# Retention attention into a top-1 mixture of experts: two matmul widths, shorter bodies and a new order of the helper steps

## The chip, the cores and the metric

The kernel runs on one core of a Trainium2 chip. The metric is the device time of one execution in microseconds, lower is better.

## The reference, cut to what matters

```python
# q, k, v: 8 batches x 8 heads x 576 positions x 64
scores = matmul(q, k.T) / sqrt(64)
gamma  = 1 - 2.0 ** (-5 - arange(8))                  # per head
ret    = scores * where(rel >= 0, gamma ** rel, 0)    # rel = row - column
x      = matmul(ret, v)  -> (4608 tokens, 512)

logits = normalize(x) @ normalize(expert_emb).T / tau
e      = argmax(logits)                               # one of 8 experts
gate   = softmax(logits)[e]
h      = maximum(x[tokens of e] @ w1[e], 0)           # 512 -> 1024
out[tokens of e] = gate * (h @ w2[e])                 # 1024 -> 512
```

## The kernel before, in words

**Attention.** 36 tiles of 128 tokens are worked in 18 steps of two tiles (`for s in range(HS)`, L858). The SyncE queue loads a tile's queries and keys (`qkt`) and its keys and values (`kvt`) into pools of seven buffers (`NLOAD = 7`). At the start of step s it loads the two tiles five ahead (L861 to L863). TensorE forms scores (`emit_A`), applies the carried state (`emit_QT`), multiplies with the values (`emit_O`) and updates the state (`emit_U`); the result is transposed (`emit_T`), copied by ScalarE into the two-buffer pool `my` and stored row by row into the scratch array `xd` (`emit_rows`). The routing of four tiles at a time is spread over later steps by a list of jobs (`at((step, place), ...)`, run by `do`).

**Between.** Once slots are known, GpSimd gathers the tokens of an expert from `xd` (`gather`), SyncE turns each gathered tile by a transposing DMA (`turn`), and a `join` puts the two 16-bit halves of each number back together. ScalarE then makes the high part of a number (`...hi`, a rounding cast) and VectorE the low part (`...lo`, number minus high part). Each product runs as three matmuls: high x high, high x low, low x high. Expert 0 is computed plainly.

**Experts 1 to 7** (L1289). The first product (512 to 1024) runs by a seven-product scheme in the manner of Strassen: sums and differences of weight quarters (`sumS1` to `sumS4`, VectorE) and of token quarters (`xsums`, VectorE), each split into high and low parts (`whi`, `wlo`, `xhi`, `xlo`). An expert's tokens lie in five tiles, each cut in two halves, so a matmul has one column for each pair of slots, 320 at most. The width is chosen at run time: the count of tokens, in steps of 16 above 512, is read into a TensorE register, and `products` writes its body once for each width of `WIDTHS`, under `tc.If` on that register (`pick`, L1033). Six calls of `products` make the 168 matmuls of an expert, in bodies of 24, 24, 48, 36, 24 and 12. Their results are turned into the hidden layer: `outs_mid`, `outs_last`, `hhi` (ScalarE, with ReLU), `hlo` (VectorE), `plus` (VectorE) and `copy` (ScalarE).

The second product (1024 to 512) is `mm2`: per tile of 128 tokens 8 blocks of 3 matmuls of 512 columns. `evac` scales by the gate on ScalarE and `scatter` (GpSimd) writes the rows out. The fifth tile runs only if the expert has more than 512 tokens (`tc.If(width > 0)`).

Within an expert all engines follow the written order of the program. While expert e runs, expert n = e + 1 is prepared between its pieces: weight quarters are loaded (`wload`, three buffers `wraw`), tokens gathered and turned, then joined on GpSimd (`join(n, i, nc.gpsimd.tensor_copy)`), summed and split. `wn` and `wnext` are the second product's weights, loaded in four parts.

Of the kernel before, what the change touches and what calls it, by code (L numbers as in the profile page):

```python
# [9 lines left out]
F32 = mybir.dt.float32  # L10
# [8 lines left out]
P = 128  # L19
# [5 lines left out]
DM = H * D  # L25
# [17 lines left out]
HW = CAP // 2  # L43
STEP = 16
WMIN = 2 * 2 * P
WIDTHS = (256, 288, 304, 320)
TOP = tuple((2 * w - WMIN) // STEP for w in WIDTHS)
KT = 9
NLOAD = 7
# [48 lines left out]
def retention_moe(ctx: ExitStack, tc: tile.TileContext, qk, kv, embT, tau, w1, w2, cst, out):  # L98
# [423 lines left out]
    with ExitStack() as att:  # L522
# [3 lines left out]
        a1 = att.enter_context(tc.tile_pool(name="a1", bufs=1))  # L526

        pmp = att.enter_context(tc.tile_pool(name="pmp", bufs=4))
        csb = ap.tile([P, _CST.shape[1] - _FIRST], F32, name="csb")
        pop = att.enter_context(tc.tile_pool(name="pop", bufs=1, space=PSUM))  # L530
        po = pop.tile([P, 2, 2, 2 * P], F32, name="po")
# [228 lines left out]

        def emit_rows(t, bank):

            xw = my.tile([P, DM], F32, name="y")
            nc.scalar.copy(
                xw.bitcast(U16).rearrange("p (h n) -> p h n", h=2),
                bank.bitcast(U16).rearrange("p (n h) -> p h n", h=2),
            )
            nc.sync.dma_start(out=xd[t * P : (t + 1) * P, :], in_=xw.bitcast(U16))
# [69 lines left out]
        for i in range(3):  # L838
            at((15, 1), lambda i=i: turn(0, i))
            at((16, 3), lambda i=i: join(0, i, nc.gpsimd.tensor_copy))  # L840
        at((17, 0), lambda: (xhi0(0), xlo0(0)))
        at((17, 1), lambda: (xhi0(1), xhi0(2), xlo0(1), xlo0(2)))

        def loads(t):
            if t < NT:
                load_qk(t)
                load_kv(t)
# [10 lines left out]
        for s in range(HS):  # L858
            t, u = 2 * s, 2 * s + 1
            do(s, 0)  # L860
            if s > 0:  # L861
                loads(t + NLOAD - 2)
                loads(u + NLOAD - 2)  # L863
            scale_v(t + 2, nc.gpsimd)
            scale_v(u + 2, nc.gpsimd)
            for k in (t + 2, u + 2):
                if k < KT:
                    decay(k)
            if 0 < s < HS - 1:
                emit_A(t + 2)  # L870
                emit_A(u + 2)
            do(s, 1)
            emit_QT(t)
            emit_QT(u)
            emit_U(u)
            emit_O(t)
            emit_O(u)
            if s == 0:
                emit_A(2)
                turn_k(2)  # L880
                emit_A(3)
                turn_k(3)
            do(s, 1.5)
            if s > 0:
                emit_T(u - 2, pa[3])
                emit_T(t - 2, prow)
            if 0 < s < HS - 1:
                emit_rows(u - 2, pa[3])
                emit_sq(u - 2, pa[3])
            emit_U(t + 2)  # L890
            emit_X(t)
            emit_X(u)
            do(s, 2)
# [29 lines left out]
    with ExitStack() as moe:  # L923
# [201 lines left out]
        gather(1, 0)  # L1125
        gather(1, 3)
        mm1_in(5, 0, q0[5])
        on(prow)
        gates_out()
        gather_gates(0)  # L1130
        out0_hi(4, 0, q0[4])
        wn.hi(1)
        out0_lo(4, 0, q0[4])
        wn.lo(1)
        turn(0, 3)
        wload(1, "A11")
        turn(0, 4)
        mm1_in(6, 0, q0[6])
        out0_hi(5, 0, q0[5])
        wn.hi(2)  # L1140
        out0_lo(5, 0, q0[5])
# [15 lines left out]
        wlo("A11")  # L1157
        join(0, 3)
        mm2(b0[0], 0, (4, 5))
        sumS3()  # L1160
        xhi0(3)
        xlo0(3)
        xg.pop((0, 3))
        gather(1, 1)
        gather(1, 4)
        mm2(b0[0], 0, (6, 7), end=7)
        evac(0, 0, b0[0])
        scatter(0, 0)
        join(0, 4)
        sumS1()  # L1170
        mm2(b0[1], 1, (0, 1), begin=0)
        whi("S3")
        xhi0(4)
        wlo("S3")
        mm2(b0[1], 1, (2, 3))
        whi("A22")
        xlo0(4)
        xg.pop((0, 4))
        gather(1, 2)
        turn(1, 1)  # L1180
        on(prow)
        count_beyond()
        mm2(b0[1], 1, (4, 5))
# [105 lines left out]
        for e in range(1, NE):  # L1289
# [25 lines left out]
            if more:  # L1315
                wload(n, "A21")
                gather_gates(n)

            products(
                width,  # L1320
                (3, 0, VA[0], 0),
                (3, 1, VA[1], 0),
                (7, 0, YA[0], 0),
                (7, 1, YA[1], 0),
                (1, 2, XB[0], 1),
                (1, 3, XB[1], 1),
                (5, 2, VB[0], 1),
                (5, 3, VB[1], 1),
            )
# [5 lines left out]
            if more:  # L1335
# [1 line left out]
                for i in range(3):  # L1337
                    turn(n, i)

            products(  # L1340
                width,
                (4, 0, YA[0], 0),
                (4, 1, YA[1], 0),
                (2, 2, XB[0], 0),
                (2, 3, XB[1], 0),
                (6, 2, YB[0], 0),
                (6, 3, YB[1], 0),
            )
            hhi(4, 0, YA[0])
            hhi(5, 0, YA[1])  # L1350
            if more:
                whi("A11")
                wlo("A11")
            hlo(4, 0, YA[0])
            hlo(5, 0, YA[1])
            outs_mid((2, 3), XB, YB)
            if more:
                sumS3()
                sumS1()
                for i in range(3):  # L1360
                    join(n, i, nc.gpsimd.tensor_copy)

            products(width, (3, 2, VB[0], 0), (3, 3, VB[1], 0), (7, 2, YB[0], 0), (7, 3, YB[1], 0))
            if more:
                outs_last((2, 3), VB, YB, lambda: whi("S1"), lambda: (wlo("S1"), sumS2("A21")))
            else:
                outs_last((2, 3), VB, YB)

            o = (bank[4], bank[5], bank[6], bank[7], bank[4])
            wnext = Split(n, 1, w2f) if more else None  # L1370
            mm2(o[0], 0, (0, 1), begin=0)
            if more:
                whi("S2")
            mm2(o[0], 0, (4, 5))
            if more:
                wlo("S2")
                whi("S3")
            products(width, (4, 2, YB[0], 0), (4, 3, YB[1], 0))
            if more:
                wlo("S3")  # L1380
                wload(n, "A12")
            hhi(6, 0, YB[0])
            hhi(7, 0, YB[1])
            hlo(6, 0, YB[0])
            hlo(7, 0, YB[1])
            mm2(o[0], 0, (2, 3))
            if more:
                xsums(n, 0)
                xhi(n, 0, "abc")
            mm2(o[1], 1, (0, 1), begin=0)  # L1390
            if more:
                xlo(n, 0, "abc")
                ready(n, 0)
                turn(n, 3)
                whi("A22")
            mm2(o[1], 1, (4, 5))
            if more:
                xsums(n, 1)
                xhi(n, 1, "abc")
            mm2(o[1], 1, (2, 3))  # L1400
            if more:
                wlo("A22")
# [6 lines left out]
            if more:  # L1409
                xsums(n, 2)  # L1410
                xhi(n, 2, "abc")
            mm2(o[1], 1, (6, 7), end=7)
            evac(e, 1, o[1])
            scatter(e, 1)
            if more:
                xlo(n, 2, "abc")
                ready(n, 2)
            mm2(o[2], 2, (0, 1), begin=0)
            if more:
                whi("A12")  # L1420
                wlo("A12")
            mm2(o[2], 2, (2, 3))
            if more:
                sumS4()
                wnext.load(0)
                whi("S4")
            mm2(o[2], 2, (4, 5))
            if more:
                join(n, 3, nc.gpsimd.tensor_copy)
                wlo("S4")  # L1430
                wnext.load(1)
                wnext.load(2)
            mm2(o[2], 2, (6, 7), end=7)
            evac(e, 2, o[2])
            scatter(e, 2)
            if more:
                xsums(n, 3)
                xhi(n, 3, "abc")
            mm2(o[3], 3, (0, 1), begin=0)
            if more:  # L1440
                join(n, 4, nc.gpsimd.tensor_copy)
                xlo(n, 3, "abc")
                ready(n, 3)
# [193 lines left out]
```

## Time and profile before

| | before |
|---|---|
| median of 3 timed runs | 614.42 us (610.39 to 614.44) |
| profiled execution | 606.46 us |
| its span, first to last instruction | 604.6 us |
| TensorE matmul busy | 566.0 us, 94%, 5156 matmuls |
| VectorE busy | 435.8 us, 72% |
| ScalarE busy | 312.1 us, 52% |
| GpSimd busy | 245.1 us, 41% |
| mean granted TensorE clock | 0.982 |

A share is the busy time over the span. Matmuls overlap in a pipeline, so 94% does not say that TensorE is at its peak. The profiled execution is one run of its own; the timed ones were taken apart from it. The attention takes about the first quarter of the span, the experts 1 to 7 from 219.5 us on.

### The profile page before, as it was taken

Reading aid. Unit: us, or ns where it says so; the run is one execution under the profiler, and the core shown is the slowest. Engines: PE = TensorE matmul, PEld = TensorE weight load, DVE = VectorE, ACT = ScalarE, POOL = GpSimd, SP = SyncE. Lnnn points to the kernel's source line nnn. Section 1 sums busy time; section 2 is a strip of 40 time slices with the busy share of each in tenths; the row PEclk is TensorE's granted clock in tenths of the full one; section 3 lists DMA queues with packets and bytes.
Section 4 is the critical chain, followed back from the end, with each engine's and each line's share of the span. In section 5 each row is a group of like instructions: output and inputs, shape, how many; then the busy total and the mean of one; then the engine's idle time right before and its main releaser. Section 6 shows DMA issues by size and latency. Waiting matters only on the chain.

```text
span 604.6 us, 13187 instructions
## 1 busy us (share of the span) xinstructions
PE 566.0 (94%) x5156; PEld 504.0 (83%) x5156; DVE 435.8 (72%) x880; ACT 312.1 (52%) x610; POOL 245.1 (41%) x218
## 2 busy tenths in 40 slices
PE   8999999999998999899899899979689999999996
PEld 7888888888887999789788878977589888889985
DVE  2777687887777777986996598759847976987500
ACT  2345454554645785537536544736465656447411
POOL 4652233226447236237525623570374137331011
PEclk9999999999998999999999899979989999999999
DMA  8898998997467549176655906572665449353001
GB/s 295 331 326 315 371 352 328 381 352 240 160 175 176 131 147 260 49 178 210 104 139 159 236 25 157 193 159 54 175 204 95 105 151 268 43 157 113 3 36 46
DMA packets 83085, 111.84 MB, mean 185 GB/s; under 512 B 48135, under 2 KB 48427, under 8 KB 82992
## 3 DMA queue, kind: packets, MB, share of 16 engines
q1 hardware_dynamic: 75312, 90.55, 51.1%
q0 software_dynamic: 7680, 19.95, 9.4%
q8 instruction: 70, 1.15, 0.8%
q14 instruction: 23, 0.19, 0.1%
HBM read 81.10 MB, written 19.94 MB: 167 GB/s over the span
## 4 chain that ended last, share of the span: by engine, by line
PE 39%; DVE 21%; issue 17%; DMA 9%; ACT 7%; POOL 3%; SPq 2%; POOLq 0%; DVEq 0%; ACTq 0%
PE pa L127 16%; PE po L127 10%; PE pst L127 6%; PE prow L127 5%; DVE w0f L989 4%; DVE graw L453 4%; DVE hs L1018 3%; DVE wraw L971 3%; DMA wraw<-w 3%; DMA qkt<-qk 2%; POOL out L1085 2%; DVE st L1031 2%; SPq L411 2%; PE pa L131 1%; DVE wxf L989 1%
## 5 line engine op out<-in xcount | busy, mean ns | idle before, releaser
L1085 POOL DMA_INDIRECT out<-y,sid x40 | 42.3, 1058 | 203.9 <-ACT y L1081 129.9
L127 PE MATMUL po<-w2f,hs 128*128 128x512 f32 x408 | 94.2, 389 | 0.0
L127 PEld LDWEIGHTS po<-w2f,hs 128*128 128x128 f32 x408 | 76.4, 188 | 15.8
L127 PE MATMUL pst<-w2f,hs 128*128 128x512 f32 (+1 forms) x336 | 80.2, 385 | 5.9 <-DVE hs L1018 4.6
L127 PEld LDWEIGHTS pst<-w2f,hs 128*128 128x128 f32 x336 | 60.4, 188 | 19.6 <-DVE hs L1018 7.2
L641 POOL TENSOR_TENSOR kvt<-kvt,cs 128x512 f32<-128x512 f32 x35 | 37.7, 1083 | 65.8 <-DMA kvt<-kv 44.4
L193 DVE TENSOR_TENSOR w2f<-wraw,w2f 128x1024 fp32r<-128x1024 f32 x32 | 39.2, 1224 | 32.2 <-ACT w2f L189 32.2
L418 POOL COPY graw<-graw 128x1024 uint16<-128x1024 uint16 x33 | 51.9, 1599 | 25.0 <-DMA graw<-graw 25.0
L986 ACT CAST w0f<-wraw 128x1024 fp32r<-128x1024 f32 x28 | 29.2, 1046 | 58.2 <-DVE wraw L971 58.2
L463 ACT CAST xxf<-graw 128x128 fp32r<-128x128 f32 x70 | 31.8, 460 | 51.4 <-DVE graw L453 51.4
L127 PE MATMUL pa<-xxf,w0f 128*128 128x256 f32 (+3 forms) x348 | 52.4, 305 | 5.3 <-ACT w2f L189 1.7
L127 PEld LDWEIGHTS pa<-xxf,w0f 128*128 128x128 f32 x348 | 49.6, 199 | 6.4 <-ACT w2f L189 1.9
L989 DVE TENSOR_TENSOR w0f<-wraw,w0f 128x1024 fp32r<-128x1024 f32 x28 | 44.8, 1600 | 12.2 <-ACT w0f L986 12.2
L658 DVE TENSOR_TENSOR pm<-pa,tri 128x512 f32<-128x512 f32 x64 | 40.1, 682 | 12.1 <-PE pa L127 12.1
L453 DVE TENSOR_TENSOR graw<-graw 128x128 f32<-128x128 f32 x140 | 44.6, 360 | 3.2 <-ACT graw L418 2.0
L397 POOL DMA_INDIRECT gt<-gd,gid x40 | 39.8, 996 | 16.7 <-issue 11.9
L127 PE MATMUL prow<-w2f,hs 128*128 128x512 f32 x192 | 46.0, 389 | 0.0
L127 PE MATMUL pa<-qkt 64*128 64x128 f32 x576 | 43.0, 284 | 2.2 <-DMA qkt<-qk 1.5
L989 DVE TENSOR_TENSOR wxf<-wraw,wxf 128x1024 fp32r<-128x1024 f32 x21 | 26.0, 1236 | 26.1 <-ACT wxf L986 26.1
L127 PEld LDWEIGHTS prow<-w2f,hs 128*128 128x128 f32 x192 | 36.0, 188 | 7.7
L971 DVE TENSOR_TENSOR wraw<-wraw 128x1024 f32<-128x1024 f32 x28 | 40.4, 1441 | 2.6 <-DMA wraw<-w 1.9
L127 PEld LDWEIGHTS pa<-qkt 64*128 64x128 f32 x576 | 38.0, 190 | 5.1 <-DMA qkt<-qk 1.8
(196 smaller groups left out, 1138.8 us busy)
## 6 DMA issues: line engine op xcount, KB each, us to landing
wraw<-w SPq DMA_DIRECT2D x64, 512.0 KB, 4.7
qkt<-qk SPq DMA_DIRECT2D x36, 512.0 KB, 7.2
kvt<-kv SPq DMA_DIRECT2D x32, 512.0 KB, 7.9
xd<-y SPq DMA_DIRECT2D x36, 256.0 KB, 4.2
kvt<-kv SPq DMA_DIRECT2D x4, 256.0 KB, 6.3
gt<-gd,gid POOLq DMA_INDIRECT x40, 5.6
out<-y,sid POOLq DMA_INDIRECT x40, 3.1
graw<-xd,gid POOLq DMA_INDIRECT x26, 5.7
```

What stands on the lines that cost most here:

```text
L127: pe[:] = [nc.tensor.matmul(*args, **kw)]
L193: nc.vector.tensor_tensor(out=self.to[:, 1, c * 1024 : (c + 1) * 1024], in0=self.raws.pop(c), in1=hi.bitcast(F32), op=ALU.subtract,)
L397: nc.gpsimd.indirect_dma_start(out=g[:, i : i + 1], out_offset=None, in_=gd[:, :], in_offset=bass.IndirectOffsetOnAxis(ap=gid[:, a : a + 1 ...
L418: copy(t[:, :DM].bitcast(U16).rearrange("p (n h) -> p h n", h=2), t[:, XO : XO + DM].bitcast(U16).rearrange("p (h n) -> p h n", h=2),)
L453: nc.vector.tensor_tensor(out=v[:, 2 * k : 2 * k + 2], in0=a, in1=b, op=ALU.subtract)
L463: nc.scalar.copy(x[:, 0], u)
L641: eng.tensor_tensor(out=v, in0=v, in1=gneg[:, t % KT].unsqueeze(2).broadcast_to([P, H, D]), op=ALU.mult)
L658: nc.vector.tensor_tensor(out=pm[:, h], in0=banks[h].rearrange("p (c n) -> p c n", c=NP), in1=m.unsqueeze(1).broadcast_to([P, NP, P]), op= ...
L971: nc.vector.tensor_tensor(out=raw[n], in0=raw[a], in1=raw[b], op=op)
L986: nc.scalar.copy(wop[n][:, 0], raw[n])
L989: nc.vector.tensor_tensor(out=wop[n][:, 1], in0=raw[n], in1=wop[n][:, 0].bitcast(F32), op=ALU.subtract)
L1085: sc = nc.gpsimd.indirect_dma_start(out=out[:, :], out_offset=bass.IndirectOffsetOnAxis(ap=sid[:, a : a + 1], axis=0), in_=ys[i], in_offse ...
```

## The change

It has six parts: two widths (296 and 320) in place of four; the calls of 48 and 36 matmuls cut into two each, so that no body exceeds 24; the joins of experts 2 to 7 on ScalarE; a new order of `hlo`, `wlo`, `whi`, `sum`, `xhi`, `xlo` and weight loads between the pieces of the second product; in the attention, loads of the next tiles written ahead of the same step's row stores, which get three buffers of their own; around expert 0, a later place for the gates and an earlier one for the last tokens' joins and parts.

```diff
-WIDTHS = (256, 288, 304, 320)
+WIDTHS = (296, 320)
...
+        rowp = att.enter_context(tc.tile_pool(name="rowp", bufs=3))
...
-            xw = my.tile([P, DM], F32, name="y")
+            xw = rowp.tile([P, DM], F32, name="xw")
...
-        at((17, 0), lambda: (xhi0(0), xlo0(0)))
-        at((17, 1), lambda: (xhi0(1), xhi0(2), xlo0(1), xlo0(2)))
+        at((17, 1), lambda: (xhi0(0), xhi0(1), xlo0(0), xlo0(1)))
+        at((17, 1.5), lambda: (xhi0(2), xlo0(2)))
...
             do(s, 0)
-            if s > 0:
-                loads(t + NLOAD - 2)
-                loads(u + NLOAD - 2)
...
                 turn_k(3)
+            if s + 1 < HS:
+                loads(t + NLOAD)
+                loads(u + NLOAD)
             do(s, 1.5)
...
-        on(prow)
-        gates_out()
-        gather_gates(0)
         out0_hi(4, 0, q0[4])
...
         wload(1, "A11")
+        mm1_in(6, 0, q0[6])
+        on(prow)
+        gates_out()
+        gather_gates(0)
         turn(0, 4)
-        mm1_in(6, 0, q0[6])
...
         mm2(b0[0], 0, (4, 5))
-        sumS3()
         xhi0(3)
+        join(0, 4)
         xlo0(3)
...
+        sumS3()
         mm2(b0[0], 0, (6, 7), end=7)
+        xhi0(4)
         evac(0, 0, b0[0])
         scatter(0, 0)
-        join(0, 4)
-        sumS1()
-        mm2(b0[1], 1, (0, 1), begin=0)
         whi("S3")
-        xhi0(4)
-        wlo("S3")
-        mm2(b0[1], 1, (2, 3))
-        whi("A22")
         xlo0(4)
...
+        mm2(b0[1], 1, (0, 1), begin=0)
+        sumS1()
+        wlo("S3")
+        whi("A22")
+        mm2(b0[1], 1, (2, 3))
...
-            products(
-                width,
-                (3, 0, VA[0], 0),
...
+            products(width, (3, 0, VA[0], 0), (3, 1, VA[1], 0), (7, 0, YA[0], 0), (7, 1, YA[1], 0))
+            products(width, (1, 2, XB[0], 1), (1, 3, XB[1], 1), (5, 2, VB[0], 1), (5, 3, VB[1], 1))
...
+            products(width, (4, 0, YA[0], 0), (4, 1, YA[1], 0), (2, 2, XB[0], 0), (2, 3, XB[1], 0))
+            products(width, (6, 2, YB[0], 0), (6, 3, YB[1], 0))
             hhi(4, 0, YA[0])
             hhi(5, 0, YA[1])
             if more:
                 whi("A11")
-                wlo("A11")
             hlo(4, 0, YA[0])
             hlo(5, 0, YA[1])
+            if more:
+                wlo("A11")
             outs_mid((2, 3), XB, YB)
             if more:
                 sumS3()
                 sumS1()
-                for i in range(3):
-                    join(n, i, nc.gpsimd.tensor_copy)
+                join(n, 0)
 
             products(width, (3, 2, VB[0], 0), (3, 3, VB[1], 0), (7, 2, YB[0], 0), (7, 3, YB[1], 0))
-            if more:
-                outs_last((2, 3), VB, YB, lambda: whi("S1"), lambda: (wlo("S1"), sumS2("A21")))
-            else:
-                outs_last((2, 3), VB, YB)
-
+            outs_last((2, 3), VB, YB)
...
+            if more:
+                whi("S1")
             mm2(o[0], 0, (0, 1), begin=0)
             if more:
-                whi("S2")
+                whi("S3")
+                wlo("S1")
+                sumS2("A21")
             mm2(o[0], 0, (4, 5))
...
             products(width, (4, 2, YB[0], 0), (4, 3, YB[1], 0))
...
             hhi(6, 0, YB[0])
             hhi(7, 0, YB[1])
+            if more:
+                whi("S2")
+                xsums(n, 0)
             hlo(6, 0, YB[0])
             hlo(7, 0, YB[1])
             mm2(o[0], 0, (2, 3))
             if more:
-                xsums(n, 0)
                 xhi(n, 0, "abc")
+                wlo("S2")
             mm2(o[1], 1, (0, 1), begin=0)
             if more:
+                join(n, 1)
                 xlo(n, 0, "abc")
                 ready(n, 0)
                 turn(n, 3)
-                whi("A22")
             mm2(o[1], 1, (4, 5))
             if more:
+                xhi(n, 1, "a")
                 xsums(n, 1)
-                xhi(n, 1, "abc")
+                xhi(n, 1, "bc")
...
                 ready(n, 2)
+                whi("A22")
             mm2(o[2], 2, (0, 1), begin=0)
             if more:
+                wlo("A22")
                 whi("A12")
+            mm2(o[2], 2, (2, 3))
+            if more:
                 wlo("A12")
-            mm2(o[2], 2, (2, 3))
-            if more:
                 sumS4()
                 wnext.load(0)
-                whi("S4")
+                wnext.load(1)
             mm2(o[2], 2, (4, 5))
             if more:
-                join(n, 3, nc.gpsimd.tensor_copy)
-                wlo("S4")
-                wnext.load(1)
-                wnext.load(2)
+                join(n, 3)
+                xhi(n, 3, "a")
+                xsums(n, 3)
+                xhi(n, 3, "bc")
...
             mm2(o[3], 3, (2, 3))
-            if more:
-                xsums(n, 4)
-                xhi(n, 4, "abc")
-            mm2(o[3], 3, (4, 5))
             if more:
                 xlo(n, 4, "abc")
                 ready(n, 4)
+                whi("S4")
+            mm2(o[3], 3, (4, 5))
+            if more:
+                wlo("S4")
+                wnext.load(2)
             mm2(o[3], 3, (6, 7), end=7)
```

The left-out pieces of the last part follow the pattern shown: each `xsums` stands between `xhi` "a" and `xhi` "bc", and `join(n, 2)` and `join(n, 4)` stand one piece of the second product before their tile's parts.

## Rows read from the trace of the kernel before

**Rows 1.** Windows, experts 1 to 7: busy us of each engine, clock, DMA.

```profile
core 0: us, PE busy (x) PEld busy (x) DVE busy (x) ACT busy (x) POOL busy (x), PEclk, DMA share, GB/s
219.50:598.60 379.10, 356.80 (x2017) 319.14 (x2016) 274.56 (x474) 200.17 (x393) 153.86 (x125) 0.98 0.51 135
```

**Rows 2.** Chain that ended last: start us, duration us, what; unbroken matmuls.

```profile
287.10 3.18 PE pa L127 x24
...
452.57 1.76 PE pa L127 x12
...
477.96 10.88 PE po L127 x48
...
511.21 3.36 PE pa L127 x24
```

**Rows 3.** TensorE's timeline, experts 3 and 4, fourth call of the first products.

```profile
336.13 1.76 PE L127 MATMUL po<-xxf,w0f 128*128 128x288 f32 x12
340.67 1.79 PE L127 MATMUL pst<-xxf,wxf 128*128 128x288 f32 x6 [2.78 <-issue]
...
345.49 1.75 PE L127 MATMUL pa<-xxf,w0f 128*128 128x288 f32 x12
...
397.10 1.64 PE L127 MATMUL pst<-xxf,wxf 128*128 128x256 f32 x6 [4.60 <-issue]
...
402.29 1.57 PE L127 MATMUL pa<-xxf,w0f 128*128 128x256 f32 x12
```

**Rows 4.** Windows: expert 4's gap and the 5.2 us behind it.

```profile
392.40:397.10 4.70, 0.10 (x1) 0.01 (x1) 2.28 (x5) 2.32 (x7) 3.79 (x4) 0.81 0.94 298
397.10:402.30 5.20, 5.20 (x25) 5.20 (x26) 0.84 (x1) 2.16 (x4) 2.49 (x4) 0.51 1.21 176
```

**Rows 5.** TensorE's timeline at the start of expert 5.

```profile
435.71 0.42 PE L127 MATMUL pa<-xsf,wxf 128*128 128x320 f32 x1 [3.94 <-ACT xsf L463]
437.40 3.30 PE L127 MATMUL pa<-xsf,wxf 128*128 128x320 f32 x11 [1.27 <-DVE xsf L468]
...
448.79 2.03 PE L127 MATMUL pa<-xxf,w0f 128*128 128x320 f32 x12 [1.66 <-ACT w2f L189]
```

**Rows 6.** TensorE's waits, 219 to 605 us: total us, times, longest.

```profile
PE pst L127 <- DVE hs L1018: 4.6, 5, 1.6
...
PE pa L127 <- ACT st L1028: 1.4, 1, 1.4
```

**Rows 7.** The page's DMA queues: packets, MB, share of 16 engines.

```profile
q8 instruction: 70, 1.15, 0.8%
```

**Rows 8.** VectorE groups by line (busy us, mean ns), then its timeline from 431 us.

```profile
L971 DVE TENSOR_TENSOR wraw<-wraw 128x1024 f32<-128x1024 f32 x28 | 40.4, 1441 | 2.6 <-DMA wraw<-w 1.9
L989 DVE TENSOR_TENSOR w0f<-wraw,w0f 128x1024 fp32r<-128x1024 f32 x28 | 44.8, 1600 | 12.2 <-ACT w0f L986 12.2
L989 DVE TENSOR_TENSOR wxf<-wraw,wxf 128x1024 fp32r<-128x1024 f32 x21 | 26.0, 1236 | 26.1 <-ACT wxf L986 26.1
...
431.99 2.71 DVE L453 TENSOR_TENSOR graw<-graw 128x128 f32<-128x128 f32 x4
...
435.99 1.01 DVE L453 TENSOR_TENSOR graw<-graw 128x128 f32<-128x128 f32 x4
```

**Rows 9.** ScalarE's joins (expert 0 and 1), by line and form.

```profile
L418 ACT COPY graw<-graw 128x1024 uint16<-128x1024 uint16 x7 | 9.5, 1358 | 0.0
```

**Rows 10.** Timelines of GpSimd and ScalarE in expert 2.

```profile
294.28 5.83 POOL L418 COPY graw<-graw 128x1024 uint16<-128x1024 uint16 x3 [3.69 <-DMA graw<-graw]
...
290.38 0.43 ACT L1028 COPY st<-pa 128x320 f32<-128x320 f32 x1 [0.37 <-PE pa L127]
```

**Rows 11.** TensorE's waits, 10 to 175 us.

```profile
PE pa L127 <- DMA qkt<-qk: 1.5, 2, 0.8
PE prow L131 <- DVE tok_all L253: 1.1, 1, 1.1
PE po L127 <- ACT T L740: 1.0, 1, 1.0
```

**Rows 12.** TensorE's timeline at expert 0's second group of tokens.

```profile
190.28 13.07 PE L127 MATMUL pa<-xxf,w0f 128*128 128x256 f32 x95 [1.59 <-DVE xxf L434]
```

More of the change, by code (lines that the diff above doesn't have):

```diff
@@ L1317, in retention_moe @@
                 gather_gates(n)
-            products(
-                width,
-                (3, 0, VA[0], 0),
[L1322 to L1329, printed above, removed]
+            products(width, (3, 0, VA[0], 0), (3, 1, VA[1], 0), (7, 0, YA[0], 0), (7, 1, YA[1], 0))
+            products(width, (1, 2, XB[0], 1), (1, 3, XB[1], 1), (5, 2, VB[0], 1), (5, 3, VB[1], 1))
             outs_last((0, 1), VA, YA, lambda: wn.hi(3), lambda: wn.lo(3))
@@ L1338, in retention_moe @@
                     turn(n, i)
[L1340 to L1348, printed above, removed]
+            products(width, (4, 0, YA[0], 0), (4, 1, YA[1], 0), (2, 2, XB[0], 0), (2, 3, XB[1], 0))
+            products(width, (6, 2, YB[0], 0), (6, 3, YB[1], 0))
             hhi(4, 0, YA[0])
@@ L1359, in retention_moe @@
                 sumS1()
-                for i in range(3):
-                    join(n, i, nc.gpsimd.tensor_copy)
+                join(n, 0)
             products(width, (3, 2, VB[0], 0), (3, 3, VB[1], 0), (7, 2, YB[0], 0), (7, 3, YB[1], 0))
-            if more:
-                outs_last((2, 3), VB, YB, lambda: whi("S1"), lambda: (wlo("S1"), sumS2("A21")))
-            else:
-                outs_last((2, 3), VB, YB)
+            outs_last((2, 3), VB, YB)
             o = (bank[4], bank[5], bank[6], bank[7], bank[4])
             wnext = Split(n, 1, w2f) if more else None
+            if more:
+                whi("S1")
             mm2(o[0], 0, (0, 1), begin=0)
             if more:
-                whi("S2")
+                whi("S3")
+                wlo("S1")
+                sumS2("A21")
             mm2(o[0], 0, (4, 5))
-            if more:
-                wlo("S2")
-                whi("S3")
-            products(width, (4, 2, YB[0], 0), (4, 3, YB[1], 0))
             if more:
@@ L1381, in retention_moe @@
                 wload(n, "A12")
+            products(width, (4, 2, YB[0], 0), (4, 3, YB[1], 0))
             hhi(6, 0, YB[0])
             hhi(7, 0, YB[1])
+            if more:
+                whi("S2")
+                xsums(n, 0)
             hlo(6, 0, YB[0])
@@ L1394, in retention_moe @@
                 turn(n, 3)
-                whi("A22")
             mm2(o[1], 1, (4, 5))
             if more:
+                xhi(n, 1, "a")
                 xsums(n, 1)
-                xhi(n, 1, "abc")
+                xhi(n, 1, "bc")
             mm2(o[1], 1, (2, 3))
             if more:
-                wlo("A22")
+                join(n, 2)
                 xlo(n, 1, "abc")
@@ L1409, in retention_moe @@
             if more:
+                xhi(n, 2, "a")
                 xsums(n, 2)
-                xhi(n, 2, "abc")
+                xhi(n, 2, "bc")
             mm2(o[1], 1, (6, 7), end=7)
@@ L1417, in retention_moe @@
                 ready(n, 2)
+                whi("A22")
             mm2(o[2], 2, (0, 1), begin=0)
             if more:
+                wlo("A22")
                 whi("A12")
-                wlo("A12")
             mm2(o[2], 2, (2, 3))
             if more:
+                wlo("A12")
                 sumS4()
                 wnext.load(0)
-                whi("S4")
+                wnext.load(1)
             mm2(o[2], 2, (4, 5))
             if more:
-                join(n, 3, nc.gpsimd.tensor_copy)
-                wlo("S4")
-                wnext.load(1)
-                wnext.load(2)
+                join(n, 3)
+                xhi(n, 3, "a")
+                xsums(n, 3)
+                xhi(n, 3, "bc")
             mm2(o[2], 2, (6, 7), end=7)
@@ L1436, in retention_moe @@
             if more:
-                xsums(n, 3)
-                xhi(n, 3, "abc")
+                xlo(n, 3, "abc")
+                ready(n, 3)
             mm2(o[3], 3, (0, 1), begin=0)
             if more:
-                join(n, 4, nc.gpsimd.tensor_copy)
-                xlo(n, 3, "abc")
-                ready(n, 3)
+                join(n, 4)
+                xhi(n, 4, "a")
+                xsums(n, 4)
+                xhi(n, 4, "bc")
             mm2(o[3], 3, (2, 3))
-            if more:
-                xsums(n, 4)
-                xhi(n, 4, "abc")
-            mm2(o[3], 3, (4, 5))
             if more:
```

## The prediction

> **What bounds the kernel now.** I read the busy shares first (TensorE 94%, VectorE 72%), then the stages, because 94% of a pipelined engine is no bound by itself. The experts 1 to 7 take 379.1 us of the 604.6, in which the granted clock is 0.98 [rows 1]. To see how much of that is work, I priced a matmul in stretches where TensorE never pauses [rows 2]: 24 of 288 columns take 3.18 us (0.1325 each), 24 of 304 take 3.36 (0.140), 12 of 320 take 1.76 (0.1467), 48 of 512 take 10.88 (0.2267). That is 0.00044 us per column, so 256 columns cost 0.118 and 296 cost 0.136 (estimates on this line). An expert has 168 first products and 5 tiles of 24 second products; a tile is 5.44 us.
>
> The routing of the reference gives experts 1 to 7 599, 567, 554, 500, 637, 579 and 582 tokens, so the widths are 304, 288, 288, 256, 320, 304, 304. Expert 4, with no more than 512, skips its fifth tile. Pure work is then 50.7 + 49.5 + 49.5 + 41.6 + 51.8 + 50.7 + 50.7 = 344.5 us. So 34.6 us of the 379.1 are lost on TensorE, and these are what the change can win. Where they lie:
> - (a) The fourth call of the first products starts late in experts 3 and 4: TensorE idles 2.78 and 4.60 us on "issue", with no releaser shown [rows 3]. Its matmuls then run slowly. The granted clock in the 5.2 us after the second gap is 0.51, the 1.2 GHz level, after TensorE had done almost nothing for 4.7 us [rows 4]. From the first of these 24 matmuls to the next group it is 4.82 us instead of 3.18 in expert 3, and 5.19 instead of 2.83 in expert 4 [rows 3]. Together 2.78 + 4.60 + 1.64 + 2.36 = 11.4 us.
> - (b) Expert 5 starts late: 3.94 us for ScalarE's high part of the tokens, 1.27 for VectorE's low part, then 47 matmuls in 9.7 us instead of 6.9, then 1.66 behind a weight split [rows 5]: 9.7 us.
> - (c) Second products wait 4.6 us in five places for low parts of the hidden layer [rows 6].
> - (d) The rest, 8.9 us in small pieces, 1.4 of it a wait for ScalarE's copies in expert 6 [rows 6].
>
> **The change, part by part.**
>
> *Two widths.* Experts 1 and 5 run at 320, the others at 296. By the prices above: +1.1 (304 to 320), +0.6 twice (288 to 296), +3.0 (256 to 296), -0.7 twice: +4.0 us, all on the path, for TensorE is the bound there.
>
> *Bodies of at most 24 matmuls.* Before, four copies of each body stand in the code, of up to 48 matmuls; TensorE jumps over three. After, two copies of at most 24. The two gaps of (a) stand right behind a 48-body, begin with no engine to wait for, and fall where DMA is busy (0.94 in the 4.7 us of the second [rows 4]); the instruction queue moved 1.15 MB in 70 packets, 16 KB each [rows 7]. I take them for code that was not there yet. Against it: the same jumps went without a gap in the other experts, so the cause needs a jump and an unlucky place in the code. The bound is 0 to 11.4 us won; I take all 11.4, since the longest jump shrinks from three copies of 48 to one of 24.
> The Trainium skill (Runtime: NRT & Kernel Launch, Instruction fetch mechanics) says that a taken branch to a target outside the window of fetched code stops the engine for a fetch, and fetches blocks of 16 KiB; the packets here have that size. The same rule speaks against this change too, since eight calls per expert now branch where six did; it is the first rival.
>
> *Joins back on ScalarE.* The joins of later experts run on GpSimd, and VectorE slows under them. The sums and low parts of the weights mean 1441 and 1600 ns, where the same size without a join beside it means 1236: 28 x 0.205 + 28 x 0.364 = 15.9 us. Four token differences took 2.71 us beside a join and 1.01 without [rows 8]. Over six experts that is 15.9 / 6 + 1.7 = 4.4 us per expert, all in the second half, where VectorE runs almost without pause. A join on ScalarE takes 1.36 us [rows 9]: 5 per expert add 6.8 us to a ScalarE that is busy 200.2 of the 379.1 us [rows 1], 28.6 per expert. So the join is hidden by ScalarE's free time, if it comes when its data is there.
> The Trainium skill (SBUF — State Buffer, Who interferes with whom) says that a VectorE instruction with two SBUF inputs and a GpSimd instruction that reads SBUF exclude each other, and ScalarE waits for neither. The 2.71 against 1.01 agrees.
>
> What it gives: in (b), expert 4's second half lacks a tile (5.44 us), so VectorE, not TensorE, ends it. Its 3.94 + 1.27 late shrink by the 4.4 to about 1. With a remnant of the slow clock I keep 2 of 9.7 (ends 0 and 6: all of the wait, without the clock's share). In the other experts the second half has 3.3 + 1.6 + 27.2 us of TensorE work, and VectorE, at 4.4 us less, ends before it.
>
> *Low parts ahead of weight splits; splits and sums behind.* The low parts of the hidden layer are what (c) waits for, and no split stands ahead of them now. Of 4.6 us I keep 0.5 (ends 0 and 4.6). What comes later instead (weight parts S2, A22, S4) is used only in the next expert, whose first calls need S1 and A11; late there would be the weights' second halves, whose loads wait for the split that frees their buffer. Two of three loads now start as a pair; I keep 4 of the 8.9 in (d).
>
> *The wait added.* ScalarE's first join now stands between the high parts of the fourth and fifth call. In expert 2 its data landed at 294.3, where GpSimd had waited 3.69 us for it, while ScalarE ended its copies at 290.8 [rows 10]. So ScalarE will stand some 3.5 us, plus the join of 1.36, with the four high parts of the fifth call queued behind. VectorE's low parts wait for these, and TensorE for the low parts. But between fifth call and first use TensorE has 12 second products (2.7 us) and 12 first products (1.6). In expert 2 the fourth call ends at 287.10 + 3.18 = 290.3 [rows 2], the fifth 24 matmuls later at 293.5, so the use is near 297.8; the join ends near 295.6, two high parts by 296.4, their low parts by 297.3. It fits by half a microsecond: cost 0, up to 5 us per expert if the data lands later.
>
> *Ahead of the experts.* "Loads ahead of row stores" puts two tiles' loads ahead of two stores on the DMA queue, where the stores wait for ScalarE's copies; TensorE waited only 1.5 us in all for loads. Moving the first high parts frees 1.0 (a state copy on ScalarE), gates behind a first product 1.1 [rows 11], and the second tile group's tokens ahead of the splits 1.6 [rows 12]. Sum 5.2. Later gates are covered by the first tile's second products. I take 4.5 (ends 1, where the weights' landing sets that start anyway, and 6); a loss is unlikely because nothing is added there.
>
> **Sum.** Of 34.6 stay 0 + 2 + 0.5 + 4 = 6.5, so 28.1 are won, less 4.0, plus 4.5: 28.6 us. The profiled execution took 606.46 (span 604.6 and 1.9 around it), so 577.9. The median of the timed runs is 614.42, 8.0 above that execution; I cannot place the difference and carry it over: 586 us.
>
> **Rivals.**
> 1. *The fetch gaps stay or move* (more branches, each with its chance of missing code). For it: 2 of 42 calls showed a gap, whatever the width; now there are 56 calls. Against: shorter jumps. Price: 11.4 us stay, 597 us. Chance 0.17.
> 2. *The second half stays bound by VectorE and ScalarE in turn*: join, difference, high part, low part now alternate between the two where GpSimd had done the join beside them. (b), (c) and (d) stay as 6 + 4.6 + 8.9 instead of 6.5: 13 us, 599 us. Against: ScalarE's 28.6 of some 54 us. Chance 0.13.
> 3. *Slower: ScalarE's first join waits for its transposed tokens in every expert.* It decides where the data lands more than about half a microsecond later than in expert 2; each further microsecond is one on the path. At 5 us in each of six experts, and with a tenth of the 30 joins of 1.36 unhidden, 30 + 4 outweigh the 28.6: 614.4 - 28.6 + 34 = 620 us. Chance 0.05.
> 4. *It wins nothing and pays the columns* (the gaps are something else and only move): 614.4 + 4.0 = 618. Chance 0.03.
>
> **Numbers.** The forecast has 0.6; two hundredths are for mixtures. Its own range is 576 (all residues gone, front at 6, part of the 8.0 gone) to 593. To leave out no more than 2 in 10, I reach up through rivals 1 and 2: 576 to 602. About 1% (6 us) is what a measurement here can tell from no change. Faster by more: forecast and rivals 1 and 2, 0.90; within 1%: 0.05; slower: 0.05.
>
> **What the profile after would show.** Only 296 and 320 columns in the experts' first products, 0.136 and 0.1467 us each in unbroken stretches; no "issue" gap ahead of a call and no clock near 0.5 after expert 1; no GpSimd join, and VectorE's sums and splits back at 1.24 us; ScalarE's first join after a DMA wait of 2 to 4 us, with no wait of TensorE behind it; the pause ahead of expert 5 at 1 to 2 us. The prediction is wrong if the gaps of (a) stand at other calls, or if TensorE waits for ScalarE's high parts right after the fifth call.

## The result, and the profile after

The changed kernel takes 587.97 us (median of 4 runs, 587.79 to 590.76) where the kernel before took 612.40 beside it (4 runs, 606.57 to 614.44): ratio 0.9629, 95% interval 0.9563 to 0.9696. The profiled execution took 590.76 us and is the longest of its four; that of before, 606.46, stands at the short end of its own, so the two profiles lie only 15.7 us apart where the medians lie 24.4. In the second set of experiments below, some executions took over 1.5% longer than the fastest of the same kernel, the profiled ones of its first two runs among them; no ratio counts them.

The page of the changed kernel, busy time of each engine and the instruction queue (packets, MB, share):

```profile
PE 565.4 (96%) x5156; PEld 505.5 (86%) x5156; DVE 406.8 (69%) x880; ACT 351.4 (60%) x640; POOL 194.5 (33%) x188
...
q8 instruction: 51, 0.84, 0.6%
```

Against the table and [rows 7]: VectorE 29 us less, ScalarE 39 more (about the 30 joins of 1.36), GpSimd 51 less, 51 instruction packets for 70. Windows over the experts 1 to 7 and over a stretch in expert 5 (columns as in [rows 1]):

```profile
219.00:583.00 364.00, 356.02 (x2017) 321.04 (x2015) 247.53 (x474) 239.43 (x424) 103.53 (x95) 0.99 0.52 139
...
443.50:447.90 4.40, 4.32 (x19) 4.32 (x20) 3.51 (x8) 3.07 (x8) 0.00 (x0) 0.61 0.43 131
```

So the experts won 15.1 us (379.1 in [rows 1]), and what lies ahead of them 0.5 (219.00 for 219.50). By the prediction's prices the work of the experts is now 344.5 + 4.0 = 348.5 us, so 15.5 of the 34.6 are still lost. TensorE's timeline shows where:

```profile
194.93 5.25 PE L127 MATMUL pa<-xxf,w0f 128*128 128x256 f32 x29 [2.73 <-DVE wraw L972]
...
422.83 0.41 PE L127 MATMUL pa<-xsf,wxf 128*128 128x320 f32 x1 [2.12 <-ACT xsf L463]
423.79 3.30 PE L127 MATMUL pa<-xsf,wxf 128*128 128x320 f32 x11 [0.55 <-DVE xsf L468]
...
439.34 0.70 PE L127 MATMUL pst<-xxf,wxf 128*128 128x320 f32 x3
440.89 0.46 PE L127 MATMUL pst<-xxf,wxf 128*128 128x320 f32 x2 [0.84 <-issue]
441.61 0.30 PE L127 MATMUL pst<-xxf,wxf 128*128 128x320 f32 x1 [0.26 <-issue]
443.58 1.52 PE L127 MATMUL prow<-xxf,wxf 128*128 128x320 f32 x6 [1.67 <-DVE st L1032]
444.90 3.13 PE L127 MATMUL pa<-xsf,w0f 128*128 128x320 f32 x12
447.87 1.92 PE L127 MATMUL pa<-xxf,w0f 128*128 128x320 f32 x12
```

- The gaps of experts 3 and 4 [rows 3] are gone. A new loss stands inside a call of 24 matmuls in expert 5, the one that begins where the fourth call began before: from 439.34 to 447.87 it takes 8.53 us for 24 matmuls of 0.1467, 3.52 us of work, so 5.0 are lost, part of it to a granted clock of 0.61. TensorE does not stop there at the start of the body, it runs one to three matmuls at a time.
- Expert 5's start waits 2.12 + 0.55 us, for 3.94 + 1.27 before [rows 5], and the weight split's 1.66 behind it is gone. Its first 23 matmuls take 4.96 us instead of 3.37, at a granted clock of 0.67: 1.6 to the clock.
- No second product waits for a low part: the 4.6 us of [rows 6] are zero.
- The wait at 194.93 belongs to expert 0's second tokens. TensorE now runs them without a wait from 186.41, for 190.28 before [rows 12], and gives the time back from 8.5 us later on: 2.73 us of wait, then 48 matmuls in 7.71 us at a granted clock of 0.78.

VectorE's groups by line (busy us, mean ns) answer to [rows 8]; the line numbers are one higher:

```profile
L972 DVE TENSOR_TENSOR wraw<-wraw 128x1024 f32<-128x1024 f32 x28 | 34.3, 1224 | 0.7
L990 DVE TENSOR_TENSOR w0f<-wraw,w0f 128x1024 fp32r<-128x1024 f32 x28 | 34.2, 1221 | 2.1 <-ACT w0f L987 1.8 <-issue 0.3
```

1441 and 1600 ns fell to 1224 and 1221, below the 1.24 us expected.

### The profile page after: what moved, and what is told of

Read it like the earlier page. It is cut to its first block, busy times and chain, and to the rows that moved or that the text cites. A ratio compares the mean times of both kernels' runs of the same rounds, so it can differ in the third digit from the quotient of the medians.

```text
span 588.9 us, 13119 instructions
## 1 busy us (share of the span) xinstructions
PE 565.4 (96%) x5156; PEld 505.5 (86%) x5156; DVE 406.8 (69%) x880; ACT 351.4 (60%) x640; POOL 194.5 (33%) x188
## 4 chain that ended last, share of the span: by engine, by line
PE 75%; issue 11%; DVE 7%; ACT 3%; DMA 2%; POOL 1%; SPq 0%; POOLq 0%; DVEq 0%; ACTq 0%
PE pa L127 26%; PE po L127 21%; PE pst L127 16%; PE prow L127 8%; PE pa L131 2%; PE prow L131 1%; POOL out L1086 1%; DMA csb<-cst 1%; DMA wraw<-w 1%; ACT graw L418 1%; DVE graw L453 1%; DVE wxf L990 1%; DVE wraw L972 1%; ACT wxf L987 1%; DVE pm L659 1%
## 5 line engine op out<-in xcount | busy, mean ns | idle before, releaser
L127 PE MATMUL pst<-w2f,hs 128*128 128x512 f32 (+1 forms) x336 | 78.5, 382 | 0.0
L127 PE MATMUL pa<-xxf,w0f 128*128 128x296 f32 (+2 forms) x348 | 52.6, 303 | 3.1 <-DVE wraw L972 2.7
L418 ACT COPY graw<-graw 128x1024 uint16<-128x1024 uint16 x37 | 50.5, 1364 | 0.9 <-DMA gt<-gd,gid 0.9
L453 DVE TENSOR_TENSOR graw<-graw 128x128 f32<-128x128 f32 x140 | 34.5, 288 | 13.0 <-ACT graw L418 11.2
L127 PE MATMUL pa<-xsf,w0f 128*128 128x296 f32 (+2 forms) x240 | 40.8, 321 | 0.0
L189 ACT CAST w2f<-wraw 128x1024 fp32r<-128x1024 f32 x32 | 33.3, 1051 | 8.8 <-DMA wraw<-w 7.8
L386 POOL DMA_INDIRECT graw<-xd,gid x26 | 30.3, 1166 | 24.3 <-DVE L_all L796 13.4
L127 PEld LDWEIGHTS pa<-xsf,w0f 128*128 128x128 f32 x240 | 38.1, 195 | 0.3 <-DVE xsf L434 0.2
```

The costliest lines, as they stand in the source:

```text
L127: pe[:] = [nc.tensor.matmul(*args, **kw)]
L189: nc.scalar.copy(self.to[:, 0, c * 1024 : (c + 1) * 1024], self.raws[c])
L386: return nc.gpsimd.indirect_dma_start(out=t[:, :DM].bitcast(U16), out_offset=None, in_=xd[:rows, :], in_offset=bass.IndirectOffsetOnAxis(a ...
L418: copy(t[:, :DM].bitcast(U16).rearrange("p (n h) -> p h n", h=2), t[:, XO : XO + DM].bitcast(U16).rearrange("p (h n) -> p h n", h=2),)
L453: nc.vector.tensor_tensor(out=v[:, 2 * k : 2 * k + 2], in0=a, in1=b, op=ALU.subtract)
```

## The experiments

All are timed beside the kernel before, on two chips: the first and the third set on one (before 604.52 and 605.85 us there), the second set on another (before 610.0). Which chip the comparison above ran on is not recorded. Ratios are compared within a set, or between the two sets of the one chip; the changed kernel itself was not timed in the second set. The times expected were put beside some 612 us, so on these chips, where the kernel before is 2 to 8 us faster, the ratios are what to hold them against.

### First set: the parts alone

*The kernel before, again.* 

> The kernel before, unchanged. Theory (code arrives late behind long jumps): TensorE's gaps on 'issue' stand again ahead of the fourth call of experts 3 and 4, for the code lies at the same places, 2 to 6 us each, and the other engines work on meanwhile. Rival (a disturbance from outside the program): the gaps stand at other calls, or all engines stop together. Time 606 to 615 us either way.

Measured 603.16 us, ratio 0.9996 (0.9969 to 1.0023). TensorE's timeline:

```profile
338.57 1.14 PE L127 MATMUL pst<-xxf,wxf 128*128 128x288 f32 x6 [2.51 <-issue]
...
394.49 1.64 PE L127 MATMUL pst<-xxf,wxf 128*128 128x256 f32 x6 [4.41 <-issue]
```

The gaps of [rows 3] come again at the same two calls out of 42, nearly as long: they belong to the program and are not the chance of one execution.

*Two widths alone.*

```diff
-WIDTHS = (256, 288, 304, 320)
+WIDTHS = (296, 320)
```

> The kernel before with the widths 296 and 320 alone; bodies of 48 and 36 stay. Theory (late code): half of the copies to jump over are gone, the gaps of experts 3 and 4 are at most half, 612 + 4 - (6 to 11) = 605 to 610 us, and the instruction queue moves about 18 packets less. Rival (the gaps come from busy DMA and not from the code's length; all of the win is in joins and order): 612 + 4 = 616 us with the gaps still there.

Measured 593.66 us, ratio 0.9815 (0.9788 to 0.9841): 10.9 us won although the columns cost 4.0 by the prediction's prices, more than expected. From start to start, experts 3 and 4 are 3.4 and 3.7 us shorter than in the kernel before again, wider columns included. TensorE's waits in the experts (total us, times, longest):

```profile
PE pst L127 <- DVE hs L1018: 7.6, 6, 1.9
PE pa L127 <- ACT xsf L463: 3.9, 1, 3.9
PE pa L127 <- DVE xsf L468: 1.1, 1, 1.1
```

No pause on issue is left, with the long bodies of 48 and 36 still there; 51 instruction packets as in the changed kernel. The waits for low parts stay, and so does expert 5's start.

*Bodies of at most 24 alone, four widths.* (The two calls cut as in the change.)

> The kernel before with the calls of 48 and 36 matmuls cut in two each; four widths stay. If the length of one body decides, the gaps are gone and the time is 612 - 11 = 601 us. If the sum of all code decides, they stay: 612 us. If each branch has its own risk, new gaps at other calls: 610 to 618 us.

Measured 593.75 us, ratio 0.981 (0.9758 to 0.9862). TensorE's timeline:

```profile
236.40 3.31 PE L127 MATMUL pa<-xxf,w0f 128*128 128x304 f32 x12 [1.85 <-issue]
...
343.96 1.87 PE L127 MATMUL po<-xxf,w0f 128*128 128x288 f32 x12 [2.15 <-issue]
...
393.79 1.67 PE L127 MATMUL pa<-xxf,w0f 128*128 128x256 f32 x12 [1.96 <-issue]
```

The gaps move to other calls, one of them to expert 1. They are shorter, and only the first is followed by the slow clock (12 matmuls of 304 columns in some 3.1 us instead of 1.68). None of the three expectations had moved gaps and a faster kernel together. A wait for an engine or for data would hardly move with the cut of a body, so this speaks for late code, that is, a body whose instructions have not arrived when TensorE jumps to it; what shows it stands under (a) below.

*Joins on ScalarE alone, at their old places.* (The joins of the fourth and fifth tile change in the same way.)

```diff
-                    join(n, i, nc.gpsimd.tensor_copy)
+                    join(n, i)
```

> The kernel before with the later experts' joins on ScalarE, at their old places. Theory (the shared port slows VectorE): VectorE's sums and low parts fall from 1441 and 1600 ns to about 1240, its busy time by some 25 us; but three joins (4.1 us) now stand ahead of the high parts of the fifth call, so TensorE waits 2 to 4 us per expert at the second products. 600 to 612 us. Rival (order, not the engine, made the win): VectorE falls as well, and the time is 612 us or more, for ScalarE's block costs what VectorE gains.

Measured 598.35 us, ratio 0.9877 (0.9837 to 0.9917). VectorE's sums and low parts, 1465 and 1634 ns in the kernel before again, fall in one edit that touches neither:

```profile
L989 DVE TENSOR_TENSOR w0f<-wraw,w0f 128x1024 fp32r<-128x1024 f32 x28 | 34.3, 1225 | 19.9 <-ACT w0f L986 19.9
L971 DVE TENSOR_TENSOR wraw<-wraw 128x1024 f32<-128x1024 f32 x28 | 34.3, 1223 | 2.5 <-DMA wraw<-w 1.8
```

Expert 5's start waits 2.25 + 0.32 us, and the gaps stay at the same calls (3.18 and 4.25).

### Second set: the changed kernel with one part undone

*Four widths and the long bodies back in the changed kernel.* 

> The changed kernel with the four widths and the bodies of 48 and 36 put back; joins and order stay changed. Theory (late code): the columns give back 4 us, the gaps of about 11 us return at the fourth call of some experts: 588 - 4 + (5 to 11) = 589 to 595 us. Rival (the gaps were no matter of the bodies): 588 - 4 = 584 us without gaps.

Measured ratio 0.9698 (0.963 to 0.9767). TensorE's timeline:

```profile
344.42 1.81 PE L127 MATMUL pst<-xxf,wxf 128*128 128x288 f32 x6 [4.25 <-issue]
...
399.66 1.64 PE L127 MATMUL pst<-xxf,wxf 128*128 128x256 f32 x6 [4.25 <-issue]
...
444.40 2.43 PE L127 MATMUL pa<-xxf,w0f 128*128 128x320 f32 x12 [2.80 <-issue]
```

With the old code the gaps are back at the two old calls, whatever the order of the helper steps, and a third stands at the third call of expert 5. The time is 0.7% above the next two kernels of the set, but the intervals overlap; as a size this run is inconclusive.

*Joins on GpSimd at the new places.* 

> The changed kernel with its five joins per expert back on GpSimd, at their new places. Theory (shared port): VectorE's differences, sums and low parts stretch again to 360, 1440 and 1600 ns, about 4 us per expert in the second half; expert 5 starts 2 to 4 us later and the others lose 0 to 2 each: 592 to 600 us. Rival (the new order alone carries it): 588 us or less, since ScalarE is freed of 6.8 us per expert.

Measured 0.9856 (0.9763 to 0.9948), from two executions of 598.74 and 605.08 us, above what was expected. Against the 0.963 of the next two runs that is 2.2% lost; whether it is more than the 1.2% the joins gave at the old places, the intervals leave open. VectorE's sums mean 1481 ns again; of the low parts those of `wxf` now stretch (1670 ns), while those of `w0f`, which the new order no longer puts beside the joins, stay at 1217. The new order puts a join only one piece of the second product ahead of its use, which would make a slower neighbour cost more; that is argued and not shown.

*Expert 0 in its old order.* 

> The changed kernel with the order around expert 0 as before (gates ahead of the seventh first product, last tokens' joins late). As the trace shows the first expert starting only 0.55 us earlier than before, the new order there won next to nothing: 587 to 590 us. If its steps each won what was estimated (1.1 and 1.6), 590 to 592 us.

Measured 0.9631 (0.9546 to 0.9715), the level of the changed kernel in its own comparison (0.9629) on a chip that may be another: no gain of the new order around expert 0 shows in the time. In the trace TensorE waits 1.49 us for VectorE, where the changed kernel does not, and runs expert 0's second tokens from 187.48, 1.1 us later than in the first profile.

*The low parts of expert 0's second tokens ahead of the count and of A22.*

```diff
-        on(prow)
-        count_beyond()
         mm2(b0[1], 1, (4, 5))
-        wlo("A22")
...
-        sumS2("A22")
-        wload(1, "A12")
...
             out0_lo(f, 1, ps)
+            if f == 0:
+                wlo("A22")
+            if f == 1:
+                sumS2("A22")
+                wload(1, "A12")
...
+        on(prow)
+        count_beyond()
         mm2(b0[2], 2, (0, 1), begin=0)
```

> The changed kernel, with the count of overflow tokens, the low part of A22 and the sum S2 moved behind the first low parts of expert 0's second token group. There TensorE waits 2.73 us for a bank that VectorE frees behind that work, and then runs 48 matmuls in 7.7 us instead of 5.7. Theory (VectorE's queue is the cause): that wait is gone and 2 to 4.5 us are won, 584 to 586 us. Rival (the turned tokens of expert 1 come too late for an earlier start): the wait moves to the joins behind, 587 to 589 us.

Measured 0.9633 (0.9566 to 0.97). The wait of 2.73 us is gone, and another stands at the start of expert 1:

```profile
219.50 0.42 PE L127 MATMUL pa<-xsf,wxf 128*128 128x320 f32 x1 [3.37 <-ACT xsf L463]
220.45 1.97 PE L127 MATMUL pa<-xsf,wxf 128*128 128x320 f32 x6 [0.54 <-DVE xsf L468]
```

The rival held: the turn of expert 1's next tile is issued at 209.95, for 207.18 in the first profile.

### Third set: do the parts add, and the changed kernel on the chip of the first set

*Two widths and joins on ScalarE, nothing else.* 

> The kernel before with the two widths and with the later joins on ScalarE at their old places; bodies, order and the front stay as before. Alone the widths gave 0.9815 and the joins 0.9877 of the time before. If the two act in different places (late code, and VectorE slowed under GpSimd), the gains add: 0.969, and what the new order of the low parts, splits and sums, the cut bodies and the front have left to give is the 0.006 up to the 0.963 of the whole change, some 4 us. Rival: the joins' gain lay under the same lost time as the widths' (a second half that ends earlier only waits for the next gap), then 0.978 or above and the order carries 1.5%. In the trace: no issue gap of 2 us or more in the experts, the start of expert 5 waits some 2.3 us for ScalarE as in the run with the joins alone, second products still wait 4 to 7 us in all for low parts of the hidden layer.

Measured 586.77 us, ratio 0.9683 (0.9633 to 0.9733): 0.9815 x 0.9877 is 0.9694, so the two add, as expected. TensorE's waits, experts 1 to 7 (total us, times, longest):

```profile
PE pst L127 <- DVE hs L1018: 5.0, 4, 1.8
PE pa L127 <- ACT xsf L463: 2.2, 1, 2.2
```

Waits for low parts are still there (7.6 us with the widths alone).

*The count behind the fourth low part.* To the run with the low parts ahead:

```diff
-        on(prow)
-        count_beyond()
         mm2(b0[2], 2, (0, 1), begin=0)
...
+            if f == 3:
+                on(prow)
+                count_beyond()
```

> The changed kernel with the second half of A22's split and its sum behind the first low parts of expert 0's second tokens, as in the run before, but the count of tokens (3.6 us of VectorE) now behind the fourth of these low parts, where VectorE waited 2.4 us, and no longer ahead of the token parts of expert 1. Theory: in the run before, the count pushed these parts back by some 3 us, the turning of the next tile with them (issued at 209.95 instead of 207.18), and so the wait of expert 1 for ScalarE. Then its pause of 3.4 and 0.5 us shrinks to under 1, expert 1 starts some 3 us earlier than in the changed kernel, near 216, and the time is 3 us (0.5%) below the changed kernel's beside it. Rival: the chain of gathers and turns on GpSimd and SyncE sets that start wherever the count stands; then expert 1 starts at 219 to 220 again and the time is that of the changed kernel.

Measured 574.82 us (572.60 to 576.55), ratio 0.9498 (0.9457 to 0.954). TensorE's timeline has no wait from expert 0's second tokens to expert 1:

```profile
192.81 5.94 PE L127 MATMUL pa<-xxf,w0f 128*128 128x256 f32 x48
198.58 5.63 PE L127 MATMUL po<-w2f,hs 128*128 128x512 f32 x24
...
214.93 2.20 PE L127 MATMUL pa<-xsf,wxf 128*128 128x320 f32 x12
```

Expert 1 starts 2.0 us earlier than in the changed kernel beside it. The median is 2.1 us lower, which agrees, though the runs overlap; so the theory is shown by the trace and not by the time.

*The changed kernel again.* 

> The changed kernel again, beside the other two on the same chip, to compare them with and to see whether its ratio of 0.963 and its lost time in the fourth call of expert 5 come again. If that lost time (single matmuls on issue, then 1.67 us for VectorE, then a slow clock, some 6 us) is late code, which depends on the layout of the program alone, it stands at the same call again; if it is a chance of the DMA traffic of that one execution, it is gone or elsewhere and the span is some 5 us shorter than the 588.9 of the first profile. Ratio 0.960 to 0.967 either way.

Measured 576.95 us (574.73 to 578.71), ratio 0.9536 (0.9495 to 0.9578), lower than I expected. TensorE's timeline:

```profile
194.73 5.96 PE L127 MATMUL pa<-xxf,w0f 128*128 128x256 f32 x48 [2.20 <-DVE hs L1000]
...
216.90 1.92 PE L127 MATMUL pa<-xsf,wxf 128*128 128x320 f32 x12
...
415.31 2.02 PE L127 MATMUL pa<-xsf,wxf 128*128 128x320 f32 x12 [1.41 <-ACT xxf L463]
```

The wait ahead of expert 5 is the only one in the experts; the lost time in that expert's fourth call is gone with the same code. So layout alone doesn't make it. Windows over the experts 1 to 7 on this chip: the kernel before, then widths and joins, then the whole change.

```profile
218.00:595.50 377.50, 355.40 (x2018) 317.54 (x2016) 275.02 (x474) 200.32 (x394) 156.09 (x125) 0.98 0.51 135
```
```profile
218.10:581.00 362.90, 354.72 (x2017) 320.42 (x2015) 247.10 (x474) 238.59 (x423) 104.90 (x95) 0.99 0.52 140
```
```profile
216.90:568.10 351.20, 349.73 (x2017) 318.21 (x2015) 247.69 (x474) 241.37 (x424) 106.65 (x95) 1.00 0.54 144
```

Widths and joins win 14.6 us of the experts, the new order and the cut bodies another 11.7. Which of those two, no run separates. The trace names 5.0 of low-part waits and about 1.4 at expert 5's start (2.25 + 0.54 against 1.41); the clock, 0.99 against 1.00, holds part of the rest.

## Why the prediction was right, and where not

The time was right, 586 for 587.97 us, and so was the ratio behind it: 586 / 614.42 is 0.954, for 0.963 in the first comparison and 0.954 in the third set. In the first comparison that is in part luck. The profile came 12.9 us above the 577.9 predicted for it (9.0 more lost in the experts, 4.0 less won ahead of them), and the 8.0 carried over, with a median 2.8 below its profile, made up for most of that. In the third set two errors cancel: 3.8 less lost in the experts, 3.3 less won ahead of them. The terms, in us lost:

| term | predicted | first profile after | third set |
|---|---|---|---|
| (a) gaps ahead of a call | 0 | 0 | 0 |
| new: single matmuls in a call of expert 5 | not foreseen | 5.0 | 0 |
| (b) start of expert 5 | 2 | 2.7 + 1.6 | 1.4 |
| (c) low parts | 0.5 | 0 | 0 |
| (d) rest | 4 | 6.2 | 1.3 |
| lost in the experts | 6.5 | 15.5 | 2.7 |
| won ahead of the experts | 4.5 | 0.5 | 1.2 |

The lost time is each window less 348.5 us; (d) is what is left over. The 1.2 is 218.07 less 216.90, the starts of expert 1.

- **(a) held.** The gaps were late code, and four copies of each body were what made it late. All four programs with four widths, bodies long or cut, joins and order old or new, have two or three gaps on issue of 1.85 us or more in the experts; of the seven with two widths none has one above 1.3 us. All twelve gaps (two traces of the kernel before, three other programs) begin at the start of a body. The trace also keeps the times of the instruction queue's packets, though not for which engine each is. Over the experts the four-width programs move 45 or 46 packets of 16 KB, those with two widths 26. In each of the twelve gaps such a packet ends, and TensorE's first matmul comes 1.3 to 1.9 us after that end. In expert 4 of the kernel before, the packet runs from 394.31 to 395.32 and the matmul of [rows 3] starts at 397.10; in expert 3 the packet ends at 339.12 and the matmul starts at 340.67. The gaps also begin while GpSimd issues the gathers of the next expert's tokens or gates. These gathers run in the programs without gaps too, so they do not make one alone, but no run moves them.
  The Trainium skill (Runtime: NRT & Kernel Launch, Instruction fetch mechanics) says that a taken branch outside the fetched window stops the engine until the target page has been fetched. The gaps agree, for they stand at jumps and a packet ends in each; the page does not say why 40 of the 42 calls pass without one.
  The first rival, gaps that move, is what cutting the bodies alone does. The step's error was to count the shorter bodies in: two widths alone remove the gaps with bodies of 48 and 36 kept.
- **Widths.** From start to start, 12 matmuls of 296 columns take 1.62 to 1.65 us in the third set's timeline of the changed kernel and 12 of 320 take 1.76: 0.135 to 0.1375 and 0.1467 each, as priced.
- **(b), (c) and the joins held.** VectorE slowed under GpSimd's joins by what was read from [rows 8], one edit took it back and its reverse brought it again. The Trainium skill (SBUF — State Buffer, Who interferes with whom) has a VectorE instruction with two SBUF inputs and a GpSimd instruction that reads SBUF exclude each other; the sums' 1465 to 1223 ns agrees. The second rival didn't come. One reading in (b) is doubtful: the 1.66 us "behind a weight split" stand ahead of a matmul that reads no `w2f`, and a packet of the instruction queue ends 1.41 us ahead of it, as in the gaps of (a). It may have been late code too; no run separates the two.
- **The wait added** cost nothing behind the fifth call, and the third rival didn't come: ScalarE's 37 joins wait 0.9 us in all for data, where I had put some 3.5 on the first of each expert; in the third set it is 3.5 in all. TensorE waits for ScalarE's copies instead, 2.2 us in three experts of the first profile, 0 in the third set.
- **The front failed.** The step added up four waits (5.2 us) and kept 4.5. They are gone: TensorE runs unbroken through expert 0's second tokens from 3.9 us sooner. But the gain at expert 1's start is 0.5 and 1.2. That removed waits add up to an earlier start was wrong. Nothing is added there, as the step said, but on VectorE the count, A22's low half and a sum stand ahead of the low parts, as they did before, and TensorE now wants these low parts sooner. VectorE's timeline of the first profile:

```profile
188.22 0.16 DVE L491 TENSOR_SCALAR ovf<-prow 128x8 f32<-128x8 f32 x1
...
192.01 1.25 DVE L990 TENSOR_TENSOR wxf<-wraw,wxf 128x1024 fp32r<-128x1024 f32 x1
193.30 1.25 DVE L972 TENSOR_TENSOR wraw<-wraw 128x1024 f32<-128x1024 f32 x1
194.47 1.07 DVE L1000 SCALAR_TENSOR_TENSOR hs<-pa,hs 128x256 fp32r<-128x256 f32 x3
```

  From 188.22 to 194.47 nothing of it is what TensorE waits for. Moving only the low parts showed the next wait, the turned tokens; moving the count as well let expert 1 start 2 us sooner.
- **The 8.0 us carried over** made the median right in the first comparison. That looks like the spread of before: on the chip of the first and third sets its profile (603.18) agrees with its median there (604.52), and so do the changed kernel's (575.91 and 576.95), within 2 us of the 577.9 predicted for a profile.

What stays open: why the changed kernel loses some 13 us more in the experts in the first profile than in the third set. From start to start, expert 5 takes 7.3 us longer, experts 2, 3 and 4 take 1.7, 1.5 and 2.1. In the first profile ScalarE too stands 2.69 us on issue up to 439.32, just before TensorE falls to single matmuls. The same lost time in the same call is in the trace with expert 0 in its old order, in the second set, and in no trace of the first and third sets. Code that comes late to several engines would be a guess, and the packets speak against it: between 437.93 and 449.83 of the first profile none is moved on the instruction queues, and none between 438.50 and 450.88 of the other. In both, GpSimd issues five gathers of gates until shortly before (441.2 and 442.2); it does so in every trace, so that is no cause shown.

## What to carry to other kernels

Where a loop body is written once per case, count the copies: fewer cases with some padding beat exact sizes here (10.9 us won net of an estimated 4.0 us of columns). A pause on issue can be held against the times of the instruction queue's packets. A helper step on an idle engine is not free if it slows the engine beside it; compare the mean duration of the neighbour's instructions with and without it. When waits ahead of a stage are removed, look at what each in-order engine has queued ahead of the next operand before counting the gain.

## What was not expected of the hardware

- The changed program differs by 11 us between two comparisons (587.97 and 576.95) where the kernel before differs by 6.5 (612.40 and 605.85).
- TensorE's first matmul came 1.3 to 1.9 us after the end of the 16 KB packet that landed in a gap, in all twelve gaps.
- A pause does not fix the clock behind it. With cut bodies, the granted clock was 0.52 in the 3.4 us behind a gap of 1.85 us, and 1.00 behind gaps of 2.15 and 1.96:

```profile
236.40:239.80 3.40, 3.40 (x14) 3.40 (x15) 3.37 (x7) 0.43 (x1) 0.73 (x1) 0.52 1.36 165
343.90:347.50 3.60, 3.54 (x26) 3.50 (x27) 2.78 (x6) 2.10 (x4) 1.53 (x1) 1.00 1.42 139
393.70:397.50 3.80, 3.71 (x31) 3.72 (x32) 3.77 (x7) 1.03 (x3) 2.39 (x3) 1.00 1.45 167
```
